# Second Fourier step in whole fp32 products, the bias added on VectorE, the weight conversion spread over more units

## The chip, the cores and the metric

The kernel runs on one core of one Trainium2 chip. The metric is the device time of one execution in microseconds; three runs of the kernel before gave 1979.81, 1980.95 and 1981.92 us, and their median, 1980.95 us, is the number to compare with. All engine times below are from one profiled execution.

## The reference

A sequence x of 4 batches, 3072 positions and 256 channels goes through a Fourier layer, then an RWKV channel mix, then a feed-forward layer with Mish. Only the Fourier layer is touched:

```python
X = np.fft.rfft(x, axis=1)
Yr = Xr @ w_r - Xi @ w_i + b_r
Yi = Xr @ w_i + Xi @ w_r + b_i
Y = sign(Y) * max(|Y| - 0.01, 0)     # real and imaginary part apart
y = np.fft.irfft(Y, n=3072, axis=1)
```

Behind it the reference has `relu(xk @ w_k)**2 @ w_v * sigmoid(xr @ w_r)` and `mish(h @ w_in) @ w_out`. The weights of these two layers arrive as float64 and are converted on the chip.

## The kernel before

The transform of 3072 = 96 x 32 points is made in two steps. The first (`s1`) multiplies blocks of x by a 96 x 96 matrix and sends the result through DRAM. The second step, the mix with the weights, the shrinkage and the first step back are a pipeline over 48 units of 256 rows (12 per batch), and one loop over `u` starts it. In iteration u the program issues, in this order: the second step of unit u+1 (`s2`), the mix of unit u (`mix`), the shrinkage of unit u, and the inverse step of unit u-2 (`is1`). Each engine works through its own instructions in program order, so the order in which this loop issues them is the order of the work.

- `s2(u+1)` is 4 products of a 128 x 128 piece of tile `A` with the constants `MC` (192 columns). The values are split into a high and a low part of type fp32r (`Ah`, `Al`, made by `split_A` on ScalarE and VectorE), so each product is three fp32r matmuls, 12 per unit. The result lies in PSUM in a tile of which there is one (tag `s2`).
- `s2_ev(u+1)` copies that PSUM tile to `Xh` (ScalarE) and subtracts to `Xl` (VectorE). The next `s2` may write the tile only then.
- `mix(u)` makes three complex-multiplication products: `k1` (6 matmuls of 256 columns), and the two halves of `mxp` (12 matmuls, with 6 more in the units with u % 12 == 6). Into `mxp` goes also one matmul of 512 columns, `SEL` by `BR`, that adds the bias. ScalarE copies `k1` to SBUF and VectorE adds both to `yt`.
- `above(u)` and `shrink(u)` make `yc` (ScalarE) and `Y` (VectorE) out of `yt`, and three GpSimd copies swap halves of `Y`. `split_Y(u-1)` makes `Yh` (ScalarE) and `Yl` (VectorE) for the inverse step of the unit before.
- In 20 iterations (`S1_AT`: u = 2 to 5, and two of every three from 8 to 30) a block of `s1` for a later batch is issued between the mix and the inverse step. I call them iterations with a stage-1 block.
- `bg(n)` does n steps of a background generator: the conversion of the weights `w_k`, `w_v` and `w_r`, 9 tiles of 12 steps (seven on VectorE, three empty, a ScalarE cast, a VectorE subtraction). It is called twice in an iteration, once behind `Xl` (in `fill`) and once at the end.
- From u = 33 on, `early(k)` does the first work of the next phase in each iteration: splits of `D`, of `IF` and of `Dp`, the prefix, the token shift.

Of the kernel before, what the change touches and what calls it, by code (L numbers as in the profile page):

```python
# [20 lines left out]
NU = B * NG  # L21
# [8 lines left out]
def kernel(  # L30
# [153 lines left out]
    FC = p1sp.tile([N1, N2, N1], F32, name="FC")  # L184
    MC = p1p.tile([128, 2, 2, 192], F32R, name="MC")
    WC = p1p.tile([128, 2, 2, 128], F32R, name="WC")
    WX = p1p.tile([128, 2, 3, 2, D], F32R, name="WX")
    BR = p1p.tile([128, 2, D], F32R, name="BR")
    SEL = p1p.tile([128, 2, 128], F32R, name="SEL")
    ZV = p1p.tile([128, 2, 2, 128], F32R, name="ZV")  # L190
# [9 lines left out]
    def load_consts():  # L200
        def t(tag):
            return p1p.tile([128, 512], F32, tag=tag, name=tag, bufs=2 if tag == "dec_raw" else 1)

        if not cst:
            cst["m"] = t("dec_raw")
            nc.sync.dma_start(out=cst["m"], in_=c_mw)
            return
        cst["x"] = [t("yt"), t("yc")]
        for v, w in zip(cst["x"], (w_r, w_i)):
            nc.sync.dma_start(out=v.rearrange("p (h n) -> p h n", h=2), in_=w.rearrange("(h p) n -> p h n", p=128))  # L210

# [32 lines left out]
    def make_bias():  # L244
        t = cst["b"]
        nc.gpsimd.tensor_copy(out=t[32:33], in_=t[0:1])
        for p in (64, 96):
            for k in range(2):
                nc.gpsimd.tensor_copy(out=t[p:p + 1, k, :], in_=t[0:1, 0, :])
        nc.scalar.copy(out=BR, in_=t)  # L250
        for p in (32, 96):
            nc.gpsimd.tensor_tensor(out=BR[p:p + 1], in0=t[p:p + 1], in1=BR[p:p + 1], op=ALU.subtract)

    def make_sel():
        t = p1p.tile([128, 512], F32, tag="Yh", name="sel", bufs=2)
        s, z = t[:, 0:256].rearrange("p (k n) -> p k n", k=2), t[:, 256:512]
        nc.gpsimd.memset(t, 0.0)
        for p in (0, 32):
            nc.gpsimd.memset(s[p:p + 1], 1.0)
            nc.gpsimd.memset(s[p:p + 1, 1, 96:97], 0.0)  # L260
            nc.gpsimd.memset(s[p + 64:p + 65, 1, 96:97], 1.0)
        nc.scalar.copy(out=SEL, in_=s)
# [43 lines left out]
    def warm(n):  # L306
        z = p1p.tile([128, 512], F32, tag="yt", name="zero", bufs=1)
# [50 lines left out]
    def split_A(u):
        h = p1p.tile([128, 2, D], F32R, tag="Ah", name="Ah", bufs=2)
        l = p1p.tile([128, 2, D], F32R, tag="Al", name="Al", bufs=2)  # L360
        split(A_t.pop(u), h, l)
        Ah[u] = (h, l)

    def s2(u):
        last = u % NG == GS
        hl = Ah.pop(u)
        p = ps1p.tile([128, 2, 512], F32, tag="s2", name="s2p", bufs=1)
        for dh in range(2):
            v = p[:, dh, 0:384].rearrange("p (c e j) -> p c e j", c=3, e=2)
            for e in range(2):  # L370
                mc = MC[:, int(last and e == 1)]
                for i, (a, w) in enumerate(((0, 0), (0, 1), (1, 0))):
                    nc.tensor.matmul(  # L373
                        out=v[:, :, e, :], lhsT=hl[a][:, e, dh * 128:(dh + 1) * 128],
                        rhs=mc[:, w, :], start=(i == 0), stop=(i == 2),
                    )
        s2_t[u] = p
# [24 lines left out]
    def mix(u):  # L402
        hl = Xh.pop(u)
        last = u % NG == GS
        p = ps1p.tile([128, 2, D], F32, tag="mx", name="mxp")
        k1 = ps1p.tile([128, D], F32, tag="k1", name="k1p", bufs=1)

        def terms(c, w):
# [302 lines left out]
    for u in range(NU + 3):  # L711
# [585 lines left out]
```

## Time and profile before

| | |
|---|---|
| median of three runs | 1980.95 us (1979.81 to 1981.92) |
| profiled execution, own time | 1983.2 us |
| its span, first to last instruction | 1981.4 us |
| mean granted TensorE clock | 0.995 of full speed |
| TensorE busy | 99% of the span |
| VectorE, ScalarE, GpSimd busy | 75%, 58%, 5% |
| iteration u = 3 begins, iteration u = 46 begins | 57.90 us, 290.10 us |

An iteration begins where the first matmul of its `s2` starts. The Fourier phase is over at about 300 us, so everything the diff touches lies in the first 15% of the span. An engine's busy share says how much of a stretch had work on it; the waits and the timeline say which engine the others waited for.

### The profile page before, as it was taken

What the parts mean: (1) busy time and instruction counts of PE and PEld (TensorE: products, weight loads), DVE (VectorE), ACT (ScalarE), POOL (GpSimd) and SP (SyncE); (2) the same over time, 40 slices, a digit from 0 to 9 for tenths busy, and PEclk for the clock granted to TensorE, in tenths of its full rate; (3) what the DMA queues carried; (4) which work ended last, traced back from release to release, by engine and by line L of the source; (5) the groups of instructions that cost most, each with busy time, mean ns of one, the idle gap of its engine ahead of it and who ended that gap; (6) DMA issues with size and microseconds to landing.
All of it is one profiled execution on the core that took longest, in us unless ns stands there. A gap on an engine that the chain in (4) does not pass through costs nothing.

```text
span 1981.4 us, 33051 instructions
## 1 busy us (share of the span) xinstructions
PE 1964.3 (99%) x12946; PEld 1862.7 (94%) x12946; DVE 1487.9 (75%) x2413; ACT 1151.6 (58%) x1765; POOL 104.2 (5%) x196
## 2 busy tenths in 40 slices
PE   8999999999999999999999999999999999999999
PEld 6899999999999999999899999999999999999998
DVE  4789787776767767775587787777787777887785
ACT  3677777777777777776544444444444444544444
POOL 1222230000000000000000000000000000000000
PEclk8999999999999999999999999999999999999999
DMA  9767432221222212110110010010000010000000
GB/s 280 208 211 219 148 109 71 66 64 51 66 62 63 65 52 67 60 54 31 38 33 22 24 31 22 22 33 23 25 30 22 22 33 22 27 28 22 22 12 22
DMA packets 71743, 123.02 MB, mean 62 GB/s; under 512 B 6370, under 2 KB 48580, under 8 KB 71588
## 3 DMA queue, kind: packets, MB, share of 16 engines
q1 hardware_dynamic: 68004, 108.33, 18.5%
q0 software_dynamic: 3584, 12.58, 1.6%
q8 instruction: 102, 1.67, 0.4%
q14 instruction: 53, 0.43, 0.1%
HBM read 70.56 MB, written 50.33 MB: 61 GB/s over the span
## 4 chain that ended last, share of the span: by engine, by line
PE 94%; DVE 2%; DMA 2%; ACT 1%; issue 1%; SPq 0%; POOL 0%; DVEq 0%; ACTq 0%; POOLq 0%
PE h L1113 20%; PE o L1161 18%; PE kp L859 14%; PE vp L897 13%; PE o L1162 9%; PE pp L836 3%; PE p L1113 3%; PE pp L540 3%; PE mxp L416 3%; PE s2p L373 2%; PE s1p L318 2%; PE k1p L416 1%; PE i1p L458 1%; PE hp L802 1%; DMA XS<-in_x_dram 1%
## 5 line engine op out<-in xcount | busy, mean ns | idle before, releaser
L1161 PE MATMUL o<-WO,gh 128*128 128x512 f32 x1536 | 562.0, 394 | 0.0
L1162 PE MATMUL o<-WO,gl 128*128 128x256 f32 x1536 | 430.3, 280 | 0.0
L1113 PE MATMUL h<-xS,WS 128*128 128x256 f32 x2208 | 350.9, 281 | 0.0
L1126 ACT COPY p1s<-p 128x256 f32<-128x256 f32 x184 | 68.5, 372 | 472.2 <-PE p L1113 470.9
L1161 PEld LDWEIGHTS o<-WO,gh 128*128 128x128 f32 x1536 | 288.9, 188 | 43.3
L1113 PEld LDWEIGHTS h<-xS,WS 128*128 128x128 f32 x2208 | 299.6, 188 | 16.1
L859 PE MATMUL kp<-xk,WK 128*128 128x384 f32 x1536 | 290.1, 337 | 0.0
L1162 PEld LDWEIGHTS o<-WO,gl 128*128 128x128 f32 x1536 | 289.5, 188 | 0.2
L897 PE MATMUL vp<-kh,WV 128*128 128x384 f32 x1024 | 281.3, 336 | 0.0
L859 PEld LDWEIGHTS kp<-xk,WK 128*128 128x128 f32 x1536 | 266.6, 188 | 0.2
L1116 DVE TENSOR_TENSOR C<-h,p1s 128x512 f32<-128x512 f32 x184 | 127.0, 690 | 157.9 <-PE h L1113 154.1
L884 DVE TENSOR_TENSOR kl<-kr,kh 128x768 fp32r<-128x768 f32 x128 | 122.8, 959 | 159.4 <-ACT kr L883 157.9
L1098 DVE TENSOR_TENSOR gl<-g,gh 128x1024 fp32r<-128x1024 f32 x184 | 223.6, 1215 | 2.1 <-ACT g L1095 2.1
L1094 ACT ACTIVATE gh<-C 128x1024 fp32r<-128x1024 f32 x184 | 195.7, 1064 | 10.8 <-DVE C L1116 10.5
L1095 ACT ACTIVATE g<-C 128x1024 f32<-128x1024 f32 x184 | 193.1, 1049 | 0.0
L1113 PE MATMUL h<-xS,WI 128*128 128x256 f32 x1104 | 189.8, 280 | 0.0
L1116 DVE TENSOR_TENSOR C<-h,wu 128x512 f32<-128x512 f32 x368 | 187.4, 551 | 0.3 <-PE h L1113 0.3
L897 PEld LDWEIGHTS vp<-kh,WV 128*128 128x128 f32 x1024 | 186.3, 188 | 0.0
L897 PE MATMUL vp<-kl,WV 128*128 128x384 f32 x512 | 171.5, 335 | 0.0
L882 ACT ACTIVATE kh<-kr 128x768 fp32r<-128x768 f32 x128 | 108.3, 846 | 89.3 <-PE vp L897 89.3
L1113 PEld LDWEIGHTS h<-xS,WI 128*128 128x128 f32 x1104 | 155.7, 188 | 0.0
L1116 DVE TENSOR_TENSOR wu<-h,C 128x512 f32<-128x512 f32 x184 | 126.5, 688 | 35.3 <-PE h L1113 31.4
(181 smaller groups left out, 3059.4 us busy)
## 6 DMA issues: line engine op xcount, KB each, us to landing
scr<-Cs SPq DMA_DIRECT2D x48, 256.0 KB
D<-scr SPq DMA_DIRECT2D x32, 384.0 KB
x2d<-r POOLq DMA_DIRECT2D x32, 384.0 KB, 3.7
x<-x2d SPq DMA_DIRECT2D x24, 512.0 KB
out_dram<-ob SPq DMA_DIRECT2D x96, 128.0 KB
A<-scr SPq DMA_DIRECT2D x44, 256.0 KB
xs<-in_x_dram SPq DMA_DIRECT2D x24, 384.0 KB
scr<-xs SPq DMA_DIRECT2D x24, 384.0 KB
```

Source lines behind the costliest of these rows:

```text
L416: nc.tensor.matmul(out=out, lhsT=a, rhs=w, start=(start and i == 0), stop=(stop and i == len(ts) - 1))
L859: nc.tensor.matmul(out=p[:, m, 0:TA], lhsT=WK[:, dh, w, f * 128:(f + 1) * 128], rhs=hl[:, v, dh, :], start=(i == 0), stop=(i == 5),)
L882: nc.scalar.activation(out=kh, in_=kr, func=AF.Square)
L884: nc.vector.tensor_tensor(out=kl, in0=kr, in1=kh, op=ALU.subtract)
L897: nc.tensor.matmul(out=p[:, o, 0:TA], lhsT=WV[:, f, w, o * 128:(o + 1) * 128], rhs=v[:, m, :], start=(f == 0 and i == 0), stop=(f == 7 and ...
L1094: nc.scalar.activation(out=gh, in_=c, func=AF.Mish)
L1095: nc.scalar.activation(out=g, in_=c, func=AF.Mish)
L1098: nc.vector.tensor_tensor(out=gl, in0=g, in1=gh, op=ALU.subtract)
L1113: nc.tensor.matmul(out=out, lhsT=a(l), rhs=xS[:, v, b, :], start=(n == 0), stop=(n == 2))
L1116: nc.vector.tensor_tensor(out=out, in0=x0, in1=x1, op=ALU.add)
L1161: nc.tensor.matmul(out=o[m], lhsT=gh[:, m2, ms], rhs=WO[:, f], start=(f == 0), stop=False)
L1162: nc.tensor.matmul(out=o[m][:, 0, :], lhsT=gl[:, m2, ms], rhs=WO[:, f, 0, :], start=False, stop=(f == 15))
```

## The change

Four edits, all in the Fourier phase.

1. `s2` multiplies `A` by `MC` as plain fp32, one product in place of three. `split_A` and its two instructions per unit are gone, and there are six `A` tiles in place of four.
2. The bias product is gone. `make_bias` makes a tile `BIAS` of 128 x 512 for both kinds of unit once, by five fp32 products and two ScalarE copies. In each unit VectorE adds `k1` (read from PSUM) and `BIAS` to `yt`, and later adds `mxp` to that. ScalarE's copy of `k1` is gone.
3. The order in an iteration is changed: `mix(u)` stands ahead of `s2_ev(u+1)`, and the second addition (`mix_ev`) stands in `above(u)`, behind `split_Y(u-1)`.
4. `bg` does 2 steps a call with a stage-1 block (3 before) and 1 in all others (1 before up to u = 32, 2 after).

```diff
     def s2(u):
...
-                mc = MC[:, int(last and e == 1)]
-                for i, (a, w) in enumerate(((0, 0), (0, 1), (1, 0))):
-                    nc.tensor.matmul(
-                        out=v[:, :, e, :], lhsT=hl[a][:, e, dh * 128:(dh + 1) * 128],
-                        rhs=mc[:, w, :], start=(i == 0), stop=(i == 2),
-                    )
+                nc.tensor.matmul(
+                    out=v[:, :, e, :], lhsT=a[:, e, dh * 128:(dh + 1) * 128],
+                    rhs=MC[:, int(last and e == 1), :], start=True, stop=True,
+                )
...
     def make_bias():
...
+        t, s = cst["b"], cst["s"]
+        for k in range(2):
+            p = ps1p.tile([128, 2, D], F32, tag="mx", name="bp")
+            nc.tensor.matmul(out=p[:, 0, :], lhsT=s[:, 0, :], rhs=t[:, 0, :], start=True, stop=True)
+            nc.tensor.matmul(out=p[:, 1, :], lhsT=s[:, k, :], rhs=t[:, 1, :], start=True, stop=(k == 0))
+            if k:
+                nc.tensor.matmul(out=p[:, 1, :], lhsT=s[:, 2, :], rhs=t[:, 0, :], start=False, stop=True)
+            nc.scalar.copy(out=BIAS[:, k], in_=p)
...
         put(k1, terms(2, 0), True)
-        nc.tensor.matmul(out=p, lhsT=SEL[:, int(last), :], rhs=BR, start=True, stop=False)
-        put(p[:, 0, :], terms(1, 2), False, False)
+        nc.vector.tensor_tensor(
+            out=t, in0=k1.unsqueeze(1).to_broadcast([128, 2, D]), in1=BIAS[:, int(last)], op=ALU.add
+        )
+        put(p[:, 0, :], terms(1, 2), True)
...
-        ks = p1p.tile([128, D], F32, tag="K1", name="K1", bufs=1)
-        nc.scalar.copy(out=ks, in_=k1)
-        t = p1p.tile([128, 2, D], F32, tag="yt", name="yt", bufs=1)
-        nc.vector.tensor_tensor(out=t, in0=p, in1=ks.unsqueeze(1).to_broadcast([128, 2, D]), op=ALU.add)
+        sums.append((t, p))
...
+    def mix_ev():
+        t, p = sums.pop()
+        nc.vector.tensor_tensor(out=t, in0=p, in1=t, op=ALU.add)
+
     def above(u):
+        mix_ev()
...
             if u > 2:
-                bg(3 if u in S1_AT else 2 if u > U_E else 1)
-
+                bg(2 if u in S1_AT else 1)
+
+        if u < NU:
+            mix(u)
         if 0 < u < NU - 1:
             s2_ev(u + 1, fill)
...
-        if 0 < u < NU - 3:
-            split_A(u + 3)
-        if u < NU:
-            mix(u)
```

VectorE's instructions of iteration 33 before, from `Y` of unit 32 to `Y` of unit 33 (the numbers behind a tile's name tell its copies apart):

```order
L439 SCALAR_TENSOR_TENSOR Y_2898<-yt_2890,yc_2896 128x512
L78 TENSOR_TENSOR Xl_2932<-s2p_2915,Xh_2931 128x768
L78 TENSOR_TENSOR Al_2938<-A_2794,Ah_2937 128x512
L428 TENSOR_TENSOR yt_2964<-mxp_2941,K1_2962 128x512
L78 TENSOR_TENSOR Yl_2967<-Y_2898,Yh_2966 128x512
L439 SCALAR_TENSOR_TENSOR Y_2972<-yt_2964,yc_2970 128x512
```

The same place in the changed kernel, with the steps of the background conversion that now fall there (L148, L150, L154). L411 is the addition of `k1` and `BIAS`, L426 the addition of `mxp`:

```order
L426 TENSOR_TENSOR yt_2358<-mxp_2356,yt_2358 128x512
L437 SCALAR_TENSOR_TENSOR Y_2392<-yt_2358,yc_2390 128x512
L148 TENSOR_SCALAR dec_b_2346<-dec_v_2345 128x512
L411 TENSOR_TENSOR yt_2420<-k1p_2419,BIAS_97 128x512
L78 TENSOR_TENSOR Xl_2441<-s2p_2410,Xh_2440 128x768
L150 SCALAR_TENSOR_TENSOR dec_b_2346<-dec_raw_2087,dec_b_2346 128x512
L78 TENSOR_TENSOR Yl_2448<-Y_2392,Yh_2447 128x512
L426 TENSOR_TENSOR yt_2420<-mxp_2418,yt_2420 128x512
L437 SCALAR_TENSOR_TENSOR Y_2454<-yt_2420,yc_2452 128x512
L154 TENSOR_TENSOR dec_v_2345<-dec_v_2345,dec_b_2346 128x512
L411 TENSOR_TENSOR yt_2481<-k1p_2480,BIAS_97 128x512
```

`Yl` of unit 32 stood between `yt` and `Y` of unit 33. Now it stands ahead of L426, the second addition of unit 33, and nothing stands between L426 and `Y` of unit 33, whose other input is ScalarE's `yc`, made of L426's result.

TensorE's instructions before, from the middle of a second step (its first six matmuls are left out) to the start of `mxp`:

```order
L373 MATMUL s2p<-MC,Ah 128x3x64 x2
L373 MATMUL s2p<-MC,Al 128x3x64
L373 MATMUL s2p<-MC,Ah 128x3x64 x2
L373 MATMUL s2p<-MC,Al 128x3x64
L416 MATMUL k1p<-WX,Xh 128x256 x2
L416 MATMUL k1p<-WX,Xl 128x256
L416 MATMUL k1p<-WX,Xh 128x256 x2
L416 MATMUL k1p<-WX,Xl 128x256
L419 MATMUL mxp<-BR,SEL 128x512
L416 MATMUL mxp<-WX,Xh 128x256 x2
```

And in the changed kernel, where each fp32 product stands as one row:

```order
L364 MATMUL s2p<-MC,A 128x3x64 x4
L408 MATMUL k1p<-WX,Xh 128x256 x2
L408 MATMUL k1p<-WX,Xl 128x256
L408 MATMUL k1p<-WX,Xh 128x256 x2
L408 MATMUL k1p<-WX,Xl 128x256
L408 MATMUL mxp<-WX,Xh 128x256 x2
L408 MATMUL mxp<-WX,Xl 128x256
L408 MATMUL mxp<-WX,Xh 128x256 x2
```

Twelve matmuls of the second step became four products, and the row of L419 (the bias, 512 columns) is gone.

## Rows read from the trace of the kernel before

**Rows 1.** The page, part 1: TensorE (PE) and its weight loads (PEld).

```profile
PE 1964.3 (99%) x12946; PEld 1862.7 (94%) x12946; DVE 1487.9 (75%) x2413; ACT 1151.6 (58%) x1765; POOL 104.2 (5%) x196
```

**Rows 2.** Windows cut where iterations u = 2, 3, 8, 31, 46 begin.

```profile
core 0: us, PE busy (x) PEld busy (x) DVE busy (x) ACT busy (x) POOL busy (x), PEclk, DMA share, GB/s
48.39:57.90 9.51, 8.01 (x43) 7.21 (x43) 6.14 (x9) 4.77 (x9) 1.94 (x4) 0.82 0.75 168
57.90:85.89 27.99, 27.99 (x202) 25.95 (x200) 20.02 (x31) 20.40 (x42) 6.70 (x15) 1.00 0.78 232
85.89:218.59 132.70, 131.85 (x929) 120.17 (x928) 117.59 (x183) 93.62 (x186) 35.22 (x69) 1.00 0.68 203
218.59:290.10 71.51, 70.47 (x544) 66.75 (x542) 60.19 (x97) 53.69 (x107) 22.79 (x45) 1.00 0.43 130
```

**Rows 3.** TensorE's timeline in one iteration: start us, us, engine, line, out<-in, count.

```profile
61.62 1.89 PE L318 MATMUL s1p<-xs,FC 96*96 96x256 f32 x8
...
64.03 0.36 PE L373 MATMUL s2p<-MC,Ah 128*128 128x192 f32 x2
...
65.35 0.42 PE L416 MATMUL k1p<-WX,Xh 128*128 128x256 f32 x2
...
66.09 0.40 PE L419 MATMUL mxp<-BR,SEL 128*128 128x512 f32 x1
66.32 0.40 PE L416 MATMUL mxp<-WX,Xh 128*128 128x256 f32 x2
66.56 0.28 PE L416 MATMUL mxp<-WX,Xl 128*128 128x256 f32 x1
```

**Rows 4.** Weight loads by line: duration min/median/max; of warm() first, then step two.

```profile
L311 PEld LDWEIGHTS warm<-zero x6: 286/337/337, 1.2 to 3.1; 128*128 128x128 f32 x6
L373 PEld LDWEIGHTS s2p<-MC,Ah x384: 186/192/333, 31.3 to 291.2; 128*128 128x128 f32 x192
```

**Rows 5.** Waits, 30 to 300 us: total us, times, longest us.

```profile
PEld s2p L373 <- DVE Xl L78: 7.7, 12, 2.1
```

**Rows 6.** Timeline of the other engines, iteration 32: start us, us, engine, line.

```profile
223.96 0.69 DVE L439 SCALAR_TENSOR_TENSOR Y<-yt,yc 128x512 f32<-128x512 f32 x1
224.53 0.80 ACT L77 CAST Xh<-s2p 128x768 fp32r<-128x768 f32 x1
224.78 0.40 POOL L441 COPY sw<-Y 64x256 f32<-64x256 f32 x1 [4.79 <-DVE Y L439]
225.37 0.96 DVE L78 TENSOR_TENSOR Xl<-s2p,Xh 128x768 fp32r<-128x768 f32 x1 [0.71 <-ACT Xh L77]
226.12 0.62 ACT L77 CAST Yh<-Y 128x512 fp32r<-128x512 f32 x1
226.24 0.68 DVE L78 TENSOR_TENSOR Al<-A,Ah 128x512 fp32r<-128x512 f32 x1
227.00 0.69 DVE L428 TENSOR_TENSOR yt<-mxp,K 128x512 f32<-128x512 f32 x1
227.60 0.68 DVE L78 TENSOR_TENSOR Yl<-Y,Yh 128x512 fp32r<-128x512 f32 x1
227.72 0.63 ACT L433 ACTIVATE yc<-yt 128x512 f32<-128x512 f32 x1 [0.97 <-DVE yt L428]
228.38 0.69 DVE L439 SCALAR_TENSOR_TENSOR Y<-yt,yc 128x512 f32<-128x512 f32 x1
```

**Rows 7.** VectorE groups, 218.59 to 290.10 us: count | busy us, mean ns | idle.

```profile
...
L78 DVE TENSOR_TENSOR Dl<-D,Dh 96x1024 fp32r<-96x1024 f32 x2 | 2.7, 1351 | 0.2 <-ACT Dh L77 0.2
L576 DVE SCALAR_TENSOR_TENSOR xf<-dl,small,yT 128x384 f32<-128x384 f32 x4 | 2.6, 683 | 0.0
L556 DVE TENSOR_TENSOR yT<-ya,s1p 128x64 f32<-128x64 f32 x12 | 1.9, 213 | 0.0
L78 DVE TENSOR_TENSOR ifh<-ift,ifh 96x384 fp32r<-96x384 f32 x2 | 1.5, 750 | 0.0
```

**Rows 8.** GpSimd's first copy of a unit: duration min/median/max.

```profile
L441 POOL COPY sw<-Y x48: 392/399/1122, 47.5 to 299.8; 64x256 f32<-64x256 f32 x48
```

More of the change, by code (lines that the diff above doesn't have):

```diff
@@ L184 @@
     FC = p1sp.tile([N1, N2, N1], F32, name="FC")
-    MC = p1p.tile([128, 2, 2, 192], F32R, name="MC")
+    MC = p1p.tile([128, 2, 192], F32, name="MC")
     WC = p1p.tile([128, 2, 2, 128], F32R, name="WC")
     WX = p1p.tile([128, 2, 3, 2, D], F32R, name="WX")
-    BR = p1p.tile([128, 2, D], F32R, name="BR")
-    SEL = p1p.tile([128, 2, 128], F32R, name="SEL")
+    BIAS = p1p.tile([128, 2, 2, D], F32, name="BIAS")
     ZV = p1p.tile([128, 2, 2, 128], F32R, name="ZV")
@@ L201, in t @@
         def t(tag):
-            return p1p.tile([128, 512], F32, tag=tag, name=tag, bufs=2 if tag == "dec_raw" else 1)
+            return p1p.tile([128, 512], F32, tag=tag, name=tag, bufs=2 if tag in ("dec_raw", "yt") else 1)
         if not cst:
@@ L221, in split_M @@
         nc.vector.memset(im[:, 1, 32:33], 0.0)
-        split(v, MC[:, :, 0, 0:128], MC[:, :, 1, 0:128])
-        split(sm, MC[:, :, 0, 128:192], MC[:, :, 1, 128:192])
+        nc.scalar.copy(out=MC[:, :, 0:128], in_=v)
+        nc.vector.tensor_copy(out=MC[:, :, 128:192], in_=sm)
     def split_W():
@@ L244, in make_bias @@
     def make_bias():
[L245 to L252, printed above, removed]
+        t, s = cst["b"], cst["s"]
[6 more added lines that the diff above has]
+            nc.scalar.copy(out=BIAS[:, k], in_=p)
     def make_sel():
         t = p1p.tile([128, 512], F32, tag="Yh", name="sel", bufs=2)
-        s, z = t[:, 0:256].rearrange("p (k n) -> p k n", k=2), t[:, 256:512]
+        s = cst["s"] = t.rearrange("p (k n) -> p k n", k=4)
         nc.gpsimd.memset(t, 0.0)
[L258 to L262, printed above, removed]
+        nc.gpsimd.memset(s[0:1, 0:2, :], 1.0)
+        nc.gpsimd.memset(s[0:1, 1, 96:97], 0.0)
+        nc.gpsimd.memset(s[0:1, 2, 96:97], 1.0)
         for h in range(2):
-            nc.scalar.copy(out=ZV[:, h], in_=z.rearrange("p (k n) -> p k n", k=2))
+            nc.scalar.copy(out=ZV[:, h], in_=s[:, 3, :].unsqueeze(1).to_broadcast([128, 2, 128]))
     def bg_small():
@@ L306, in warm @@
     def warm(n):
-        z = p1p.tile([128, 512], F32, tag="yt", name="zero", bufs=1)
+        z = p1p.tile([128, 512], F32, tag="yt", name="zero", bufs=2)
         nc.vector.memset(z[:, 0:256], 0.0)
@@ L348, in gview @@
         return scr.rearrange("s n d -> (s n) d")[256 * g:256 * (g + 1)].rearrange("(e p) d -> p e d", e=2)
-    A_t, Ah, Xh, Yh = {}, {}, {}, {}
+    A_t, Xh, Yh = {}, {}, {}
+    NAB = 6
     def load_A(u):
         b, g = divmod(u, NG)
-        t = p1p.tile([128, 2, D], F32, tag="A", name="A", bufs=4)
+        t = p1p.tile([128, 2, D], F32, tag="A", name="A", bufs=NAB)
         nc.sync.dma_start(out=t, in_=gview(scr1a if u < 4 else scr1[b], g))
         A_t[u] = t
[L358 to L362, printed above, removed]
     def s2(u):
         last = u % NG == GS
-        hl = Ah.pop(u)
+        a = A_t.pop(u)
         p = ps1p.tile([128, 2, 512], F32, tag="s2", name="s2p", bufs=1)
@@ L406, in mix @@
         k1 = ps1p.tile([128, D], F32, tag="k1", name="k1p", bufs=1)
+        t = p1p.tile([128, 2, D], F32, tag="yt", name="yt", bufs=2)
         def terms(c, w):
@@ L423, in mix @@
             ts += [(ZV[:, a, dh, :], WX[:, dh, 0, b, :]) for dh in range(2) for (a, b) in ((0, 0), (0, 1), (1, 0))]
-        put(p[:, 1, :], ts, False)
-        ks = p1p.tile([128, D], F32, tag="K1", name="K1", bufs=1)
-        nc.scalar.copy(out=ks, in_=k1)
-        t = p1p.tile([128, 2, D], F32, tag="yt", name="yt", bufs=1)
-        nc.vector.tensor_tensor(out=t, in0=p, in1=ks.unsqueeze(1).to_broadcast([128, 2, D]), op=ALU.add)
+        put(p[:, 1, :], ts, True)
+        sums.append((t, p))
         mx_t[u] = t
+    sums = []
+    def mix_ev():
+        t, p = sums.pop()
+        nc.vector.tensor_tensor(out=t, in0=p, in1=t, op=ALU.add)
     def above(u):
+        mix_ev()
         up = p1p.tile([128, 2, D], F32, tag="yc", name="yc", bufs=1)
@@ L467, in is1_ev @@
         p = i1_t.pop(u)
-        tag, n = ("Cs", 2) if u < NU - 3 else ("A", 4)
+        tag, n = ("Cs", 2) if u < NU - 3 else ("A", NAB)
         st = p1p.tile([128, 2, D], F32, tag=tag, name="Cs", bufs=n)
@@ L618 @@
     s1(1, 2)
-    split_A(0)
-    split_A(1)
     s1_ev()
@@ L631 @@
     split_mix()
+    s1(1, 3)
     make_bias()
-    s1(1, 3)
     store_kept(0)
@@ L642 @@
     s2_ev(1)
-    split_A(2)
     load_A(4)
     split_W()
-    split_A(3)
     WK = pkp.tile([128, 2, 2, FK], F32R, tag="WK", name="WK", bufs=1)
@@ L751 @@
         if u > 2:
-            bg(3 if u in S1_AT else 2 if u > U_E else 1)
+            bg(2 if u in S1_AT else 1)
         if u == U_E:
```

## The prediction

> **What bounds the kernel now.** I read the page first. TensorE is busy for 99% of the span [rows 1], so over the whole kernel nothing but TensorE's own work seems to count. That is an average, and the diff touches only the Fourier phase, so the next view is the busy time by stage. In iterations 3 to 7, 8 to 30 and 31 to 45 TensorE is busy for 27.99 of 27.99, 131.85 of 132.70 and 70.47 of 71.51 us at full clock; only iteration 2 has a hole, 1.50 of 9.51 us, at a granted clock of 0.82 [rows 2]. The waits agree: on the other engines' last word before the next second step, `Xl`, TensorE's weight loads waited 7.7 us in all, 12 times [rows 5]. So today each iteration lasts as long as its matmuls, and VectorE, with 117.59 of 132.70 us and 60.19 of 71.51 us, is close behind [rows 2]. The question is whether VectorE's new order still fits under a shorter TensorE iteration.
>
> **TensorE's part.** The bias product starts at 66.09 and the matmul behind it at 66.32 [rows 3]: 0.23 us for 512 columns. One in each of 48 units is gone, 11.0 us. A second step lasts from 64.03 to 65.35, 1.32 us for 12 matmuls [rows 3]. What it costs in fp32 is not in the trace of that line, but stage 1 is in fp32 already: 4 products are 8 matmul records, and 8 records last 1.89 us, of which the last, 0.38 us long like a lone 512-column one, drains; (1.89 - 0.38) / 7 = 0.216 us a record at 256 columns. Two fp32r matmuls of 256 columns take 0.24 us and one of 512 takes 0.23 [rows 3], so time goes by columns: 0.162 us a record at 192 columns, and 8 records are 1.30 us. The bounds are 0.86 us (all 8 at the 0.11 us pace of today's twelve) and 1.73 us (0.216 us each, no gain from fewer columns). I take 1.30, since the row is the same kind of matmul: 0.02 x 48 = 1.0 us. TensorE's floor per iteration falls by 0.25 us, 12 us in all. From the timeline's iterations of 6.13 and 4.43 us it becomes 5.88 us with a stage-1 block and 4.18 without.
>
> The Trainium skill, TensorE: Matmul & The Clock Gate, section on the weight-path perf modes, says that fast weight loading is on only when the input is not FP32, and puts its gain at about 2x. The trace does not show such a difference: at the lower clock a weight load of 128 fp32 columns took 337 ns at most, and the fp32r loads of the second step 333 ns at most [rows 4]. By the rule a load could outlast the 0.162 us record; by the rows it stays hidden, and my sum goes by the rows.
>
> **VectorE's part.** Counting instructions, nothing changes: `Al` goes, the addition of `k1` and `BIAS` comes, both 128x512, and VectorE's pace for such a one is 0.60 us (`yt` at 227.00, `Yl` at 227.60) [rows 6]. The order does change, and I follow one unit through it:
>
> - From `Y` of a unit to its `Yh` on ScalarE, with three GpSimd copies between: 223.96 to 226.12, 2.16 us. `Yh` lasts 0.62, and VectorE starts some 0.04 us behind ScalarE (`Xh` ends at 225.33, `Xl` starts at 225.37). So `Yl` can start 2.82 us behind `Y` [rows 6].
> - `Yl` to the second addition, 0.60 us.
> - From that addition to `yc` on ScalarE: 227.00 to 227.72, 0.72 us; from `yc` to `Y`: 227.72 to 228.38, 0.66 us [rows 6].
>
> Before, `yt` stood ahead of `Yl`, and `Yl` filled VectorE's wait for `yc`; `Yl` of one unit and `yt` of the next did not depend on one another. Now `Yl` of unit u-1, the addition of unit u, `yc` and `Y` of unit u stand in one line, and `Y` of unit u starts the next round. That ring closes no faster than 2.82 + 0.60 + 0.72 + 0.66 = 4.80 us an iteration. With a stage-1 block (5.88 us) it has 1.1 us to spare. Without one it is longer than TensorE's 4.18, and longer than today's 4.43.
>
> Between `Y` and the next `Yl` VectorE has to place `Y` 0.61, the new addition 0.60, `Xl` 0.87 (225.37 to 226.24) [rows 6], 2.08 of the 2.82 us. Everything else must fit into 0.74 us or it lengthens the ring. The whole occupies VectorE for 2.08 + 0.60 + 0.72 + 0.66 = 4.06 us an iteration, the wait for `yc` included, since nothing may run in it.
>
> **What else stands in that gap.** A step of the weight conversion: iterations 8 to 30 have 117.59 us of VectorE [rows 2], less 23 x 3.4 for the five standing instructions (0.87 + 4 x 0.60 and their tails), 39 us for the 97 steps done there, 0.4 us a step. And from u = 33 the first work of the next phase: two `Dl` of 1.35 us, four `xf` of 0.68, twelve `yT` of 0.21, two `ifh` of 0.75 [rows 7], with `delta`, `xk` and two small ones 10.6 us back to back. Counting 119 steps at 4 a stage-1 iteration and 2 in others, 25 are left for u = 31 to 43; before, all were done by u = 28.
>
> **The sum, by stretch.**
>
> - *To 57.90 us.* Five fp32 products of 256 columns are new on TensorE, 10 records of 0.216 us, 2.2 us, or 4.3 at half clock. The 1.50 us hole of iteration 2 goes: there ScalarE stood at a split of `A` whose load had not landed, with the copy of `k1` behind it, and neither exists any more; with it part of what the lower clock cost behind it (8.01 us busy where 6.13 is usual, 1.9 us) [rows 2]. I take -1 us, bounds -3.5 and +2.
> - *u = 3 to 30*, 160.7 us now. TensorE's floor is 19 x 5.88 + 9 x 4.18 + 3 x 0.72 (six extra matmuls in three units) = 151.5. VectorE needs 28 x 4.06 + 94 x 0.4 = 151.3. Two engines that both need all the time and hand work to each other lose some on both; steps come in clusters. I take 155.7: -5 us, bounds -9 (TensorE's floor) and -1 (half of what is lost on each wait comes back as another).
> - *u = 31 to 47.* No stage-1 blocks are left. VectorE needs 15 x 4.06 + 10.6 + 25 x 0.4 = 81.5 us for the 15 iterations that last 71.51 [rows 2]. The ring counts each iteration by itself, the larger of 4.80 and 4.06 plus its own extras, which is 1 to 3 us more, and two more units at 4.80 in place of less than 4.5 add 0.6. GpSimd's copies, 0.40 us, took up to 1.12 us where `Dl` ran beside them [rows 8], and they are a part of the ring. I take +12.5 us, bounds +8 and +15.
>
> 1983.2 (the profiled execution's time) - 1 - 5 + 12.5 = 1989.7 us. That execution lies 2.25 us above the median of the runs, so 1987.5 on their scale; I say **1987**.
>
> **The rivals.**
>
> *TensorE stays the bound* (faster). Then the 12 us of its floor come off, 1969 us. It needs the ring to close in 4.18 us, which the rows of its links forbid as long as `Yl` stands ahead of the addition; it decides in iterations 31 to 45, from the point where the ring's 4.80 is overstated by 0.6. A smaller form: the best end of all three stretches, -3.5 - 9 + 8 = -4.5, 1976.5. Chance 0.09.
>
> *The two cancel* (no change). Stretch two gives 8, the start 2, and stretch three costs 9 to 10: 1980 to 1982. For it speaks that TensorE's floor and VectorE's need in stretch two are so near that I can't read the loss off any row. Chance 0.25.
>
> *The clock falls.* With TensorE idle for 1 to 1.5 us in many iterations of stretch three it may be granted 1.2 GHz, as in iteration 2, where the clock was 0.82 on average and the busy time 1.9 us longer [rows 2]. TensorE has that time to spare there, but not in a row: 3 to 5 such places cost 5 to 8 us more, 1994. Chance 0.06.
>
> *fp32 weight loads are slow*, 0.216 us a load: the second step takes 1.73 us, 0.41 more, in the 31 iterations in which TensorE has no slack, 13 us: 2000. The loads' row speaks against it [rows 4]. The Trainium skill's rule on fast weight loading, named above, is this one. Chance 0.03.
>
> **How the numbers follow.** My own case has 0.57 and gives 1982 to 1993. A difference under 0.2%, 4 us, can hardly be told from none. Faster by more than that: 0.09. Same: 0.27, the cancelling case and the low edge of mine. Slower: 0.64, the rest of mine with the clock and the loads. The range reaches from the best ends (about 1977) to the clock case: 1978 to 1995.
>
> **What would show it.** In the changed kernel's trace the second step should last 1.30 us, with no row of 512 columns in the mix. Iterations with a stage-1 block should last about 5.9 us, those from u = 31 on 4.8 us and more, 5.5 on average, with VectorE waiting for `yc` some 0.7 us in each of them and TensorE waiting for `Xl` ahead of `s2`, 10 us or more in all. If iterations 31 to 33 last 4.2 us, the ring is wrong. If they last 4.8 and the stretch is still no longer than now, the extras hide where I don't see it. If stretch two is at 151 us, I have overstated what two near-equal engines lose.

## The result and the profile after

The changed kernel takes 1996.71 us (median of five runs, 1995.53 to 1998.94) against 1980.95 us: a ratio of 1.0084, 95% interval 1.0071 to 1.0096. It is slower by 15.8 us. I had said 1987 us, slower by 6, and 1995 as the upper end: the sign was right and the size wrong. The profiled execution took 1998.43 us, 15.2 more than that of before.

The first part of the changed kernel's page, against [rows 1]:

```profile
PE 1958.3 (98%) x12716; PEld 1853.9 (93%) x12716; DVE 1482.2 (74%) x2412; ACT 1114.3 (56%) x1668; POOL 96.4 (5%) x186
```

TensorE has 6 us less work than before in a span that is 15 us longer, and VectorE also 6 us less. So no engine got more to do. The time went into waits. Where, the windows of the changed kernel say. They are cut where u = 3, 8, 31 and 46 begin, then at 312.40, where the last but one inverse step begins, at the next phase's first `kp` (316.69) and its first `pp` (322.35); columns as in [rows 2]:

```profile
57.45:84.06 26.61, 26.61 (x177) 24.73 (x176) 18.57 (x30) 16.65 (x33) 6.11 (x15) 1.00 0.81 236
84.06:216.28 132.22, 126.65 (x814) 114.54 (x814) 108.17 (x169) 74.25 (x137) 33.39 (x69) 1.00 0.66 199
216.28:299.54 83.26, 68.96 (x468) 63.46 (x467) 69.38 (x117) 44.56 (x82) 24.03 (x45) 1.00 0.41 122
299.54:312.40 12.86, 8.80 (x59) 7.72 (x59) 8.63 (x13) 6.04 (x11) 3.11 (x6) 1.00 0.13 42
312.40:316.69 4.29, 4.26 (x15) 3.36 (x15) 3.00 (x15) 2.71 (x10) 1.20 (x3) 0.57 0.33 111
316.69:322.35 5.66, 5.66 (x26) 5.66 (x24) 2.47 (x3) 3.79 (x6) 0.00 (x0) 0.72 0.72 210
```

And of before, the two stretches behind [rows 2], with the same meaning (`kp` at 303.11, `pp` at 307.28):

```profile
298.99:303.11 4.12, 3.00 (x14) 2.20 (x15) 2.95 (x14) 3.03 (x11) 1.19 (x3) 1.00 0.19 64
303.11:307.28 4.17, 4.17 (x25) 4.16 (x24) 2.91 (x6) 3.76 (x6) 0.00 (x0) 1.00 0.78 224
```

| stretch | before | after | difference | forecast |
|---|---|---|---|---|
| to u = 3 | 57.90 | 57.45 | -0.5 | -1 |
| u = 3 to 7 and 8 to 30 | 160.69 | 158.83 | -1.9 | -5 |
| u = 31 to 45 | 71.51 | 83.26 | +11.8 | +11.9 |
| from u = 46 to `kp` | 13.01 | 17.15 | +4.1 | +0.6 |
| `kp` to `pp` | 4.17 | 5.66 | +1.5 | 0 |
| behind it | 1674.1 | 1674.0 | -0.1 | 0 |

So two terms are off: the gain of u = 3 to 30 is missing by 3, and the end of the phase, which I had priced at 0.6, costs 5.6.

VectorE and ScalarE in iteration 32 of the changed kernel, a stretch of its timeline that answers [rows 6]:

```profile
222.92 0.69 DVE L437 SCALAR_TENSOR_TENSOR Y<-yt,yc 128x512 f32<-128x512 f32 x1 [0.76 <-ACT yc L431]
...
223.53 0.42 DVE L140 TENSOR_SCALAR dec_v<-dec_raw 128x512 int32<-128x512 int32 x1
...
223.86 0.68 DVE L411 TENSOR_TENSOR yt<-k1p,BIAS 128x512 f32<-128x512 f32 x1
...
224.46 0.95 DVE L78 TENSOR_TENSOR Xl<-s2p,Xh 128x768 fp32r<-128x768 f32 x1
...
225.33 0.68 DVE L144 SCALAR_TENSOR_TENSOR dec_v<-dec_raw,dec_v 128x512 int32<-128x512 int32 x1
...
225.51 1.54 PE L364 MATMUL s2p<-MC,A 128*128 128x192 f32 x8 [0.66 <-PE i1p L456]
225.93 0.69 DVE L78 TENSOR_TENSOR Yl<-Y,Yh 128x512 fp32r<-128x512 f32 x1
226.53 0.68 DVE L426 TENSOR_TENSOR yt<-mxp,yt 128x512 f32<-128x512 f32 x1
226.75 0.53 PE L408 MATMUL k1p<-WX,Xh 128*128 128x256 f32 x2
...
227.31 0.63 ACT L431 ACTIVATE yc<-yt 128x512 f32<-128x512 f32 x1 [1.53 <-DVE yt L426]
...
227.97 0.69 DVE L437 SCALAR_TENSOR_TENSOR Y<-yt,yc 128x512 f32<-128x512 f32 x1 [0.76 <-ACT yc L431]
```

Read VectorE's starts downwards: it goes from one instruction to the next without a hole until L426 at 226.53, whose result ScalarE turns into `yc`. Then it stands until 227.97. Only 0.76 us of that is marked as idle, since L426 is counted as busy until 227.21, but nothing else starts for 1.44 us. From `Y` to `Y` it is 5.05 us, of which TensorE works 4.4; TensorE's 0.66 us ahead of `s2` is put down to `i1p`, the instruction before it on its own engine, though what ended last is `Xl` (224.46 + 0.95 = 225.41). The waits of the changed kernel, 30 to 320 us, columns as in [rows 5]:

```profile
DVE Y L437 <- ACT yc L431: 36.1, 48, 0.8
...
PEld s2p L364 <- PE i1p L456: 11.3, 10, 1.4
PEld s2p L364 <- issue: 11.0, 8, 2.3
...
PEld s2p L364 <- DVE Xl L78: 2.9, 2, 2.2
```

The wait for `yc` is in every one of the 48 units. Ahead of the second step TensorE's weight loads waited 25 us in these three groups, where they had waited 7.7 for `Xl` [rows 5]. Two of the groups are put down to TensorE itself; that `Xl` ended last is read above for iteration 32, and not shown for each of the others.

### The profile page after: what moved, and what is told of

It is laid out like the page before. It is cut to its first block, busy times and chain, and to the rows that moved or that the text cites. A ratio compares the mean times of both kernels' runs of the same rounds, so it can differ in the third digit from the quotient of the medians.

```text
span 1996.3 us, 32502 instructions
## 1 busy us (share of the span) xinstructions
PE 1958.3 (98%) x12716; PEld 1853.9 (93%) x12716; DVE 1482.2 (74%) x2412; ACT 1114.3 (56%) x1668; POOL 96.4 (5%) x186
## 4 chain that ended last, share of the span: by engine, by line
PE 92%; DVE 4%; ACT 1%; issue 1%; DMA 1%; SPq 0%; POOL 0%; ACTq 0%; POOLq 0%; DVEq 0%
PE h L1105 20%; PE o L1153 18%; PE kp L851 14%; PE vp L889 13%; PE o L1154 9%; PE pp L828 3%; PE p L1105 3%; PE pp L538 3%; PE s1p L315 2%; PE s2p L364 2%; PE mxp L408 2%; PE i1p L456 1%; PE k1p L408 1%; PE hp L794 1%; DVE Xl L78 1%
```

## The experiments

Eleven kernels ran, in three batches beside runs of the kernel before (medians 1980.13, 1980.33 and 1980.61 us). The stretch up to u = 3 differs by some 3 us between single executions of kernels that have the same code there (57.45 in the changed kernel, 54.67 with the old step counts), so single executions are compared by the stretches behind it, and by these names:

| kernel | ratio to before, 95% | u = 3 to 7 | 8 to 30 | 31 to 45 | 46 to `kp` | `kp` to `pp` |
|---|---|---|---|---|---|---|
| before | | 27.99 | 132.70 | 71.51 | 13.01 | 4.17 |
| after | 1.0084 [1.0071, 1.0096] | 26.61 | 132.22 | 83.26 | 17.15 | 5.66 |
| Yl between | 0.9974 [0.9964, 0.9983] | 26.61 | 124.32 | 73.43 | 13.94 | 6.16 |
| old step counts | 1.0120 [1.0105, 1.0135] | 31.30 | 141.43 | 77.80 | 16.81 | 5.06 |
| both of these | 0.9991 [0.9982, 1.0001] | 28.45 | 128.79 | 69.03 | 13.94 | 4.89 |
| no swaps | 1.0050 [1.0033, 1.0066] | 26.61 | 130.14 | 82.14 | 14.64 | 4.19 |
| fp32 alone | 0.9975 [0.9965, 0.9985] | 27.80 | 129.81 | 69.31 | 13.52 | 5.05 |
| bias alone | 1.0177 [1.0162, 1.0192] | 28.93 | 151.58 | 81.05 | 15.30 | 5.10 |
| mix behind | 1.0095 [1.0078, 1.0112] | 26.61 | 134.78 | 84.95 | 17.90 | 4.98 |
| no conversion | 1.0011 [1.0002, 1.0020] | 26.61 | 124.32 | 77.81 | 17.13 | 5.79 |
| more steps early | 0.9974 [0.9962, 0.9985] | 28.22 | 127.11 | 69.03 | 13.95 | 5.91 |
| bias, mix ahead | 1.0091 [1.0077, 1.0104] | 28.30 | 141.73 | 73.95 | 13.27 | 4.17 |
| bias without Al | 1.0048 [1.0034, 1.0062] | 27.27 | 137.97 | 70.65 | 15.13 | 5.29 |

**Yl between.** The main theory: VectorE's wait for `yc`, which nothing fills, is the cause. So the second addition is issued ahead of the split of the unit before, and `Yl` fills the wait:

```diff
     def above(u):
-        mix_ev()
...
+        if u < NU:
+            mix_ev()
         if 1 <= u <= NU:
             split_Y(u - 1)
```

> The second addition (L426) goes ahead of Yl in VectorE's order; all else as in the changed kernel. Theory A, VectorE's order: the changed kernel's VectorE waits 36.1 us for yc, 0.76 us in each of 48 units, with nothing it may do meanwhile; with Yl (0.60 us) in that place an iteration needs 3.46 us of VectorE and not 4.06. Then iterations 31 to 45 go from 83.26 us to about 73, iterations 3 to 30 from 158.8 to about 153.5, and the drain behind iteration 46 from 17.1 to about 13 with no half-clock start of the next phase: some 20 us less, 1976 to 1979 us. Theory B, the conversion steps moved into iterations 31 to 43 (10 us of VectorE) are what costs: no more than 5 us less, 1991 or above.

Measured: 1974.3 us, 22 less than the changed kernel and a quarter of a per cent faster than before. That is theory A and 2 us more than its range: u = 3 to 30 gained more than it said (150.93 us against 153.5), while the low clock behind the phase, which it had ending, stayed (`kp` to `pp` takes 6.16). Its VectorE from `Y` to `Y`, in the place of the timeline above:

```profile
212.83 0.69 DVE L436 SCALAR_TENSOR_TENSOR Y<-yt,yc 128x512 f32<-128x512 f32 x1 [0.16 <-ACT yc L430]
...
215.84 0.69 DVE L426 TENSOR_TENSOR yt<-mxp,yt 128x512 f32<-128x512 f32 x1
216.44 0.68 DVE L78 TENSOR_TENSOR Yl<-Y,Yh 128x512 fp32r<-128x512 f32 x1
217.28 0.69 DVE L436 SCALAR_TENSOR_TENSOR Y<-yt,yc 128x512 f32<-128x512 f32 x1 [0.16 <-ACT yc L430]
```

The same instructions, one pair exchanged: 4.45 us in place of 5.05, the difference being the 0.60 that `Yl` no longer takes outside the wait. And its windows for u = 8 to 30 and 31 to 45, and its wait for `yc`:

```profile
82.78:207.10 124.32, 124.32 (x814) 115.39 (x813) 108.65 (x170) 76.60 (x138) 33.22 (x69) 1.00 0.72 214
207.10:280.54 73.44, 67.93 (x469) 63.30 (x467) 68.11 (x115) 43.50 (x80) 23.96 (x45) 1.00 0.45 133
```

```profile
DVE Y L436 <- ACT yc L430: 7.2, 42, 0.7
```

VectorE's busy time is what it was in the changed kernel (108.65 against 108.17 us in u = 8 to 30), yet the stretch is 8 us shorter and TensorE works through all of it. So the loss goes when the order alone is changed and the load stays. The load has a share in it all the same, as no conversion shows below.

**Old step counts**, and **both**: the conversion's counts put back, in the changed order and in that of Yl between.

```diff
-                bg(2 if u in S1_AT else 1)
+                bg(3 if u in S1_AT else 2 if u > U_E else 1)
...
-            bg(2 if u in S1_AT else 1)
+            bg(3 if u in S1_AT else 2 if u > U_E else 1)
```

> Only the number of conversion steps a call goes back to that of before (3, 2, 1); VectorE's order as in the changed kernel. Theory A: iterations 31 to 45 lose 10 us of conversion but can't go under 4.80 us each plus the first work of the next phase, about 78 us in place of 83.3; iterations 3 to 30 get those steps on top, 3 us more; the drain stays as it is: 1993 to 1996 us. Theory B: iterations 31 to 45 go back to 71 us or less and the whole to 1980 to 1984 us.

> Both together: the second addition ahead of Yl, and the conversion steps of before. Theory A: iterations 31 to 45 at about 69 us (TensorE's own 67.8), iterations 3 to 30 at about 154, the drain at 13: 1972 to 1976 us, some 3 us under the first experiment. Theory B: about as the run with the steps of before alone, 1980.

Measured: 2004.29 and 1978.89 us. On the whole the spread of the conversion is no part of the loss; the old counts cost 8 us in the changed order and 5 in the other, although u = 31 to 45 gets 5.5 and 4.4 shorter by them. Both expectations were too low: the steps that return to u = 3 to 30 cost 13.9 us there in the changed order and 6.3 in the other, since VectorE is the bound of more iterations than I thought.

**No swaps.** The ring of the prediction, `Y`, three GpSimd copies, `Yh`, `Yl`, addition, `yc`, `Y`, against VectorE's occupation with the wait in it: both predict a slow stretch from u = 31 on. Without the copies the ring is short and the occupation as it was.

```diff
-        w = p1p.tile([64, D], F32, tag="sw", name="sw", bufs=1)
-        nc.gpsimd.tensor_copy(out=w, in_=y[64:128, 0, :])
-        nc.gpsimd.tensor_copy(out=y[64:128, 0, :], in_=y[0:64, 1, :])
-        nc.gpsimd.tensor_copy(out=y[0:64, 1, :], in_=w)
```

> The three GpSimd copies that swap the halves of Y are left out, so that part of the computation is missing; the ring Y, GpSimd, Yh, Yl, second addition, yc, Y gets 1.4 us shorter, while VectorE's own occupation of 4.06 us an iteration stays. If the length of the ring sets the pace in most iterations, 31 to 45 fall by about 12 us and the drain by 4: 1980 us. If VectorE's occupation with the unfilled wait sets it, only the waits of Yl for Yh go (9.3 us in 14 places) with part of the drain: 1986 to 1989 us.

Measured: 1989.96 us, a microsecond above the range that the occupation gave. Of the 11.8 us lost in u = 31 to 45 the copies give back 1.1: there the occupation sets the pace. In the phase's end they give back 2.5 of 4.1: there the ring has the larger part, for VectorE has little else to do.

**No conversion.** VectorE's load in the changed order, without the weight conversion's part:

```diff
-            yield from bg_weight(pool, src, hi, lo, f, raw=raw)
+            for _ in range(10):
+                yield
+            h = raw[:, :, 1].bitcast(F32)
+            h = h if f is None else h.rearrange("p (f n) -> p f n", f=f)
+            nc.scalar.copy(out=hi, in_=h)
+            yield
+            nc.scalar.copy(out=lo, in_=h)
+            yield
```

> The changed kernel without VectorE's part of the weight conversion (two plain ScalarE casts of the raw words take its place, so w_k, w_v and w_r are not converted rightly): VectorE loses 29 us in iterations 8 to 30 and 9 us in 31 to 45. Theory A: VectorE needs 4.1 us and the ring 4.80, so in iterations 8 to 30 TensorE is the bound but for the 7 iterations without a stage-1 block: 125 to 128 us in place of 132; in 31 to 45 the ring and the first work of the next phase leave 75 to 77 in place of 83: 1982 to 1986 us. If the loss in iterations 8 to 30 had another cause than VectorE's load, they stay at 130 or above.

Measured: 1982.74 us, as theory A had it. Its window for u = 8 to 30:

```profile
83.16:207.48 124.32, 124.32 (x815) 115.35 (x814) 82.06 (x118) 79.14 (x144) 27.30 (x69) 1.00 0.71 212
```

To the hundredth that is the time of Yl between, under the 125 to 128 that the theory gave, since the 7 iterations without a block are at TensorE's 4.15 too. So the wait for `yc` alone does no harm there, and neither do the steps alone: it takes both to lose 8 us.

**Mix behind.** The other half of the new order, alone put back: the mix behind the eviction of the next second step, as before.

```diff
-        if u < NU:
-            mix(u)
         if 0 < u < NU - 1:
             s2_ev(u + 1, fill)
...
+        if u < NU:
+            mix(u)
```

> The changed kernel with the mix put back behind the evacuation of the second step, so that Xl stands ahead of the addition of k1 and BIAS again; Yl stays ahead of the second addition. Theory A (the unfilled wait for yc and VectorE's occupation): the wait stays 36 us, nothing much is won: 1993 to 1999 us. Rival C (the new addition, which waits for TensorE's k1, holds up Xl and with it the next second step): iterations 8 to 30 win 4 to 7 us: 1988 to 1992 us.

Measured: 1999.83 us, 3 more than the changed kernel; the two intervals of the ratio overlap. The mix ahead is at most a small gain, and the theory that its new place cost the time falls.

**fp32 alone, bias alone.** The two main edits by themselves on the kernel before, of each the main lines: first the fp32 second step (no `split_A`, six `A` tiles), then the bias on VectorE, where the second addition stands ahead of `Yl` as in Yl between and the mix stays behind the eviction.

```diff
-                mc = MC[:, int(last and e == 1)]
-                for i, (a, w) in enumerate(((0, 0), (0, 1), (1, 0))):
-                    nc.tensor.matmul(
-                        out=v[:, :, e, :], lhsT=hl[a][:, e, dh * 128:(dh + 1) * 128],
-                        rhs=mc[:, w, :], start=(i == 0), stop=(i == 2),
-                    )
+                nc.tensor.matmul(
+                    out=v[:, :, e, :], lhsT=a[:, e, dh * 128:(dh + 1) * 128],
+                    rhs=MC[:, int(last and e == 1), :], start=True, stop=True,
+                )
```

```diff
-        nc.tensor.matmul(out=p, lhsT=SEL[:, int(last), :], rhs=BR, start=True, stop=False)
+        nc.vector.tensor_tensor(
+            out=t, in0=k1.unsqueeze(1).to_broadcast([128, 2, D]), in1=BIAS[:, int(last)], op=ALU.add
+        )
```

> The kernel before with the second step in fp32 alone (its splits gone, six A tiles); bias product, order and conversion steps as before. The second step should last 1.30 us in place of 1.32, 1 us over 48 units, and VectorE has 0.60 us an iteration less, so the few stalls of before go too: 1976 to 1980 us. If the fp32 product cost more than its row of stage 1 says (0.216 us a record, 1.73 us a unit), 20 us more: 2000.

> The kernel before with the bias on VectorE alone: the addition of k1 and BIAS where the matmuls of k1 stand in before's order, the second addition ahead of Yl, the second step in three fp32r products with its splits, conversion steps as before. TensorE's floor falls by 11.2 us, VectorE's need rises from 3.46 to 4.06 us an iteration by the work itself, without any unfilled wait. By the rule that in each iteration the longer of the two engines counts, iterations 8 to 30 stay at about 131 us and 31 to 45 at about 72: 1976 to 1981 us, so that the gain of the product is eaten by VectorE also in the good order. If only the unfilled wait matters, 1969 to 1973 us.

Measured: 1975.76 and 2016.01 us. fp32 is a gain of 4.6 us. The bias alone lies 35 us above the upper end of its first expectation and 43 above that of the second, so a third cause had to be found. Its window for u = 8 to 30:

```profile
87.59:239.17 151.58, 135.91 (x905) 119.85 (x906) 133.09 (x205) 87.68 (x163) 34.87 (x69) 0.98 0.60 177
```

VectorE is busy for 133.09 us, 15.5 more than before [rows 2]: it has six standing instructions, for `Al` is still there and the new addition has come. Two more kernels take that apart.

**Bias, mix ahead**, and **bias without Al**:

```diff
+        if u < NU:
+            mix(u)
         if 0 < u < NU - 1:
             s2_ev(u + 1, fill)
...
-        if u < NU:
-            mix(u)
```

```diff
         h = p1p.tile([128, 2, D], F32R, tag="Ah", name="Ah", bufs=2)
-        l = p1p.tile([128, 2, D], F32R, tag="Al", name="Al", bufs=2)
-        split(A_t.pop(u), h, l)
-        Ah[u] = (h, l)
+        if u == 0:
+            Ah["l"] = p1p.tile([128, 2, D], F32R, tag="Al", name="Al", bufs=1)
+            split(A_t.pop(u), h, Ah["l"])
+        else:
+            nc.scalar.copy(out=h, in_=A_t.pop(u))
+        Ah[u] = (h, Ah["l"])
```

> The bias alone (three-product second step, Yl between the additions, step counts of before), and now the mix issued ahead of the second step's eviction, as in the changed kernel. Theory of load: with Al back VectorE has six standing instructions, the first addition must wait for Xl of its own unit wherever it stands, and the order of the two changes little: 2008 to 2016 us. Theory of order: the 35 us of the bias alone came from the first addition standing behind the next unit's Xl and Al, which held k1's PSUM tile and so TensorE; with the mix ahead most of it is gone: 1980 to 1990 us.

> The bias alone as in the run that gave 2016 us, but Al is made once, for unit 0, and every later second step multiplies by that old tile, so the second step's numbers are wrong and TensorE's work, ScalarE's Ah and the order are all as there: only 47 subtractions of 128x512 on VectorE are left out. Theory of load: VectorE is the bound in nearly every iteration, each is shorter by the subtraction's 0.61 us and what Al waited for Ah, 28 to 36 us in all: 1980 to 1988 us. Theory of order: Al had slack and little comes back, 2005 to 2014 us.

Measured: 1998.62 and 1989.95 us, 17.4 and 26.1 less than the bias alone, each between its two theories. Load and order both count. The same window of the second, where VectorE has 21 instructions fewer:

```profile
84.61:222.58 137.97, 130.30 (x906) 116.09 (x906) 120.28 (x184) 88.19 (x164) 34.30 (x69) 1.00 0.66 197
```

12.8 us less of VectorE's time made the stretch 13.6 us shorter, as one expects where VectorE is the bound. The clock has a share too: it was 0.98 in the first window and 1.00 in the second, and the same matmuls kept TensorE busy for 135.91 us and 130.30. The bias needs the fp32 step, which frees the place on VectorE that the bias takes. "Both of these" is the kernel of bias, mix ahead with the fp32 second step: 1978.89 us against 1998.62.

**More steps early.** Yl between, with three steps at the end of an iteration with a stage-1 block, so that fewer are left from u = 31 on:

```diff
-            bg(2 if u in S1_AT else 1)
+            bg(3 if u in S1_AT else 1)
```

> Yl between the two additions as in the run that moved the second addition, and three steps of the weight conversion instead of two at the end of each iteration with a stage-1 block, so that fewer are left for u = 31 on. If VectorE's load sets the pace from u = 31 on and TensorE that of u = 8 to 30, the 16 steps done earlier cost nothing there (124.3 us, VectorE has 5.9 us an iteration) and take 16 x 0.37 us = up to 6 us off the stretch u = 31 to 45 (73.4): 67.5 to 71 us, 1969 to 1973 us in all. If VectorE is a bound in u = 8 to 30 as well, as when both parts of the step counts were put back (128.8 us there), it gives 2 to 4 us back there: 1973 to 1976 us.

Measured: 1975.84 us, the same ratio as without it. Stretch 31 to 45 lost 4.4 us as the first theory had it (69.03), and u = 3 to 30 gave 4.4 back. In u = 8 to 30 the 16 iterations with a block, where the steps were put, grew by 0.03 us on average, and six of the seven without one from 4.15 to 4.52. So the load was paid for in the next short iteration.

By the ratios Yl between, this kernel and fp32 alone can't be told apart (0.9974, 0.9974, 0.9975). The bias on VectorE shows no gain on top of the fp32 step in any order that ran: the 6.7 us by which Yl between is shorter than fp32 alone in u = 3 to 30 go again in u = 31 to 45 (4.1), behind it (1.5) and in the start.

## Why the prediction was wrong

**TensorE's part was right.** The floor of an iteration, forecast at 4.18 us without and 5.88 with a stage-1 block, is 4.15 and 5.87 in Yl between. The second step, from its first matmul to `k1`, takes 1.24 us in the rows above (225.51 to 226.75) where I had taken 1.30 and it had been 1.32. By the kernel with fp32 alone it is a gain: its iterations without a block last 4.39 us against 4.43 where nothing held them up before. The rival of slow fp32 loads falls: in the changed kernel a load of the second step lasts 190 ns in the median, and 192 before [rows 4].

```profile
L364 PEld LDWEIGHTS s2p<-MC,A x384: 186/190/333, 32.4 to 300.6; 128*128 128x128 f32 x192
```

The Trainium skill, TensorE: Matmul & The Clock Gate, section on the weight-path perf modes, has fast weight loading on only when the input is not FP32. These rows show no longer load for fp32 than for fp32r.

**Stretch 31 to 45 was right**: 83.26 us, forecast 83.4; 5.55 us an iteration, forecast 5.5. So was its mechanism, with a finer point. The ring is a floor: of 47 distances from `Y` to `Y` in the changed kernel none is below 4.80 us, the sum of its links, and without the swaps the shortest is 3.43. But only one is at 4.80, and two of the distances in u = 31 to 45 are at 5.05, the others longer, as VectorE's occupation has it. So the ring adds little to the occupation: no swaps gives back 1.1 us, the low end of the 1 to 3 that I gave it. Iteration 31 lasts 4.17 us by TensorE's count, and I had said that 4.2 in iterations 31 to 33 would refute the ring. It doesn't: 32 and 33 last 5.05, and from `Y` to `Y` unit 31 took 5.69. I take it that TensorE's count may be short for one iteration where the one before it left VectorE ahead.

**The term of u = 3 to 30 failed**, and the step is the comparison of two sums. I wrote "TensorE's floor is 19 x 5.88 + 9 x 4.18 + 3 x 0.72" and "VectorE needs 28 x 4.06 + 94 x 0.4", found 151.5 and 151.3, and guessed 4 us for what two near-equal engines lose. But the sums hide that the bound changes from iteration to iteration. Iterations of the changed kernel and of Yl between, from first matmul of `s2` to the next (us; * has a stage-1 block):

| u | 8* | 9* | 10 | 11* | 12* | 13 | mean of 16 with | mean of 7 without |
|---|---|---|---|---|---|---|---|---|
| after | 5.89 | 6.05 | 4.83 | 5.94 | 6.09 | 5.12 | 6.03 | 5.11 |
| Yl between | 5.88 | 5.86 | 4.15 | 5.86 | 5.87 | 4.15 | 5.96 | 4.15 |

With a block TensorE sets the time, without one VectorE does: two steps of conversion and the five standing instructions, 4.06 + 2 x 0.4 = 4.86 us, against TensorE's 4.18. What VectorE has left over in the long iterations did not shorten the short ones; I put that down to the one PSUM tile of `s2`, which no run changed. The sum over iterations of the larger of the two, from my own numbers, is 19 x 5.88 + 9 x 4.86 + 3 x 0.72 = 157.6; measured 158.83. That it comes so close is partly luck: u = 6 and 7, without a block, stay at TensorE's floor (u = 3 to 7 takes 26.61 us in the changed kernel and in Yl between alike), the other seven take 5.11 in place of 4.86, and those with a block 6.03 in place of 5.96. That no conversion and Yl between reach the same 124.32 us shows it from both sides: take away either the steps or the unfilled wait and the short iterations are TensorE's again.

**The end of the phase failed** by more: "two more units at 4.80 in place of less than 4.5 add 0.6". The last three `Y` of before and of the changed kernel, by VectorE's timeline:

```profile
291.34 0.69 DVE L439 SCALAR_TENSOR_TENSOR Y<-yt,yc 128x512 f32<-128x512 f32 x1
295.56 0.69 DVE L439 SCALAR_TENSOR_TENSOR Y<-yt,yc 128x512 f32<-128x512 f32 x1
298.99 0.68 DVE L439 SCALAR_TENSOR_TENSOR Y<-yt,yc 128x512 f32<-128x512 f32 x1
```

```profile
301.43 0.69 DVE L437 SCALAR_TENSOR_TENSOR Y<-yt,yc 128x512 f32<-128x512 f32 x1 [0.76 <-ACT yc L431]
307.02 0.69 DVE L437 SCALAR_TENSOR_TENSOR Y<-yt,yc 128x512 f32<-128x512 f32 x1 [0.76 <-ACT yc L431]
311.90 0.69 DVE L437 SCALAR_TENSOR_TENSOR Y<-yt,yc 128x512 f32<-128x512 f32 x1 [0.76 <-ACT yc L431]
```

Their distances were 4.22 and 3.43 us, far under the 4.5 of my term, and are 5.59 and 4.88: 2.8 us. Another 0.65 lies ahead of the first of the three (1.24 us behind the start of u = 46 before, 1.89 now), and 0.67 between the last and `kp` (4.12 and 4.79). By my own ring the two distances give 9.6 - 7.65 = +2.0; I had not looked at the rows of the end. That the ring has the larger part in it shows in no swaps, which takes 2.5 us off the stretch.

**The clock** was a rival with 0.06, put in the wrong place: from u = 31 to 45 it stays at 1.00, and it falls behind the last units. In the windows of the changed kernel it is 0.57 from 312.40 to 316.69 and 0.72 from there to 322.35, means over stretches at 1.2 and at 2.4 GHz, and that first stretch of `kp` takes 5.66 us in place of 4.17: 1.5 us.

**The other terms**: the start gave -0.5 for -1, within what it varies. Of the rivals, that the two cancel is refuted with its term, and TensorE as the bound is what Yl between shows for u = 3 to 30: its 150.93 us are at the floor of 151.5.

Left open: of the bias alone, order (17.4 us) and `Al` (26.1 us) were each taken away, and both together only along with the fp32 step (both of these, 37.1 us less than the bias alone). One by one they give 43.5, so they overlap by 6 us or more, if the rest of the fp32 step costs nothing there. And why the start varies was not followed.

## What to carry to other kernels

A wait on another engine in the middle of an engine's program is load of that engine, as much as an instruction, unless something independent stands behind the producer to fill it: here exchanging two instructions (second addition and `Yl`) was worth 22 us, more than leaving out the whole conversion (14 us) or the three copies (7 us) in the same kernel. Where two engines are near each other, don't compare their sums over a stretch but take the larger in each iteration, and do the same at the end of a pipeline, where the neighbours that hid a chain have gone. And two edits that trade places on one engine are judged together: the bias on VectorE lost 18 to 36 us by itself, and with the fp32 step, which took `Al` away, and in the best order it came out no faster than the fp32 step alone.

## What the runs showed of the hardware

A hole of TensorE in the last units can cost twice, by its own length and by the clock behind it. These are the changed kernel's second-last inverse step and Yl between's, with the idle time ahead of it in brackets:

```profile
312.39 0.50 PE L456 MATMUL i1p<-Yh,WC 128*128 128x512 f32 x1 [3.04 <-ACT Cs L468]
```

```profile
290.14 0.50 PE L455 MATMUL i1p<-Yh,WC 128*128 128x512 f32 x1 [1.38 <-ACT Cs L467]
```

Behind the first the clock was 0.57 and 0.72 in the windows of the section on the result. Behind the second, in the windows of Yl between to its `kp` and from there to `pp`, it was 0.70 and 0.65, though the hole was 1.38 us alone:

```profile
290.30:294.48 4.18, 3.89 (x14) 2.90 (x15) 2.97 (x15) 2.46 (x9) 1.19 (x3) 0.70 0.33 111
294.48:300.64 6.16, 6.16 (x25) 6.16 (x24) 2.32 (x3) 3.96 (x6) 0.00 (x0) 0.65 0.73 215
```

Before, the holes ahead of the last two inverse steps were 0.66 and 0.51 us, and the clock stayed at 1.00. But the length of this one hole doesn't decide it: in bias, mix ahead it was 1.39 us, as in Yl between, and `kp` to `pp` ran at full clock:

```profile
312.90 0.50 PE L463 MATMUL i1p<-Yh,WC 128*128 128x512 f32 x1 [1.39 <-ACT Cs L475]
```

```profile
316.62:320.79 4.17, 4.17 (x25) 4.16 (x24) 2.91 (x6) 3.75 (x6) 0.00 (x0) 1.00 0.79 229
```

What does decide it no run here shows. Yl between loses 2 us in `kp` to `pp` (6.16 against 4.17), which no run tried to get back.

GpSimd's copies are stretched by some of VectorE's work beside them: the first of a unit took 396 ns at least, 468 in the median and 1123 at most in the changed kernel, where the median had been 399 [rows 8]. Without VectorE's part of the conversion, in no conversion, the median is 397. They are links of the ring; here the changed kernel, then no conversion:

```profile
L439 POOL COPY sw<-Y x48: 396/468/1123, 50.0 to 312.7; 64x256 f32<-64x256 f32 x48
```

```profile
L446 POOL COPY sw<-Y x48: 392/397/1117, 49.1 to 298.4; 64x256 f32<-64x256 f32 x48
```

I had put the longest copies down to `Dl` beside them. The first copy of 1.12 us before, at 282.31, began beside `xk`, and only its end ran beside `Dl`:

```profile
282.22 0.96 DVE L78 TENSOR_TENSOR xk<-xf,xk 128x768 fp32r<-128x768 f32 x1
282.31 1.12 POOL L441 COPY sw<-Y 64x256 f32<-64x256 f32 x1 [2.87 <-DVE Y L439]
283.17 1.34 DVE L78 TENSOR_TENSOR Dl<-D,Dh 96x1024 fp32r<-96x1024 f32 x1
```
